# V's bound sent to all partitions by one matmul, and a new instruction order for attention and two MLPs

## The chip, the cores and the metric

The kernel runs on one core of a Trainium2 chip. The metric is device time in microseconds (us), from launch to end, as the median of several runs. The core has five engines with a queue each: TensorE (PE, matmuls), VectorE (DVE), ScalarE (ACT), GpSimd (POOL) and SyncE (SP, which here only starts transfers). Each works through its own instructions in program order and waits for the others by semaphores. PE's clock is granted by a throttle, at 1.2 or 2.4 GHz; the profile writes 0.5 and 1.0 for these.

## The reference

Attention with pooled queries, then an MLP with a leaky ramp, then an MLP with a rational function:

```python
q_pool = q.reshape(B, H, S // 2, 2, D).mean(axis=3)          # B=2, H=8, S=1152, D=64
scores = (1 / np.sqrt(D)) * np.matmul(q_pool, k.transpose(0, 1, 3, 2))
attn = np.exp(scores - scores.max(axis=-1, keepdims=True))
attn = attn / (attn.sum(axis=-1, keepdims=True) + 1e-09)
x = np.matmul(attn, v)                                        # -> 1152 tokens x 512
h = x @ w_in                                                  # 512 x 2048
x = (np.maximum(h, 0) + alpha * np.minimum(h, 0)) @ w_out     # 2048 x 512
h = x @ w_in2
P = a[0] + a[1] * h + a[2] * h**2 + a[3] * h**3
Q = 1 + abs(b[0]) * abs(h) + abs(b[1]) * h**2
out = (P / (Q + 1e-6)) @ w_out2
```

## The kernel before

**Numbers.** The matmuls keep nearly full float32 precision: an operand is split into a high part and a rest, and a product is three matmuls (high by high, high by rest, rest by high).

**Attention.** The 16 heads (2 batches of 8) run as 8 pairs `p`; head `2p` is the even one, `2p+1` the odd one. A head has 576 pooled queries and 1152 keys. For a pair, SP loads q, k and v (`load_q`, `load_k`, `load_v`); POOL adds the two query rows of a pool (`q_sum`) and forms a difference of keys (`k_diff`); ACT and DVE split q and k (`q_hi`, `q_lo`, `k_hi`, `k_lo`); SP's moves, all at L816, bring the parts to the tiles that PE reads: `qh_move` and `ql_move` into `QQ`, `k1_move` (two transfers) and `k2_move` into `K`. Then PE makes a first round of cheap scores for a bound on the maximum of each row (`max_mm`, with the parts `(p, j, chunks)`, read by `max_1` and `max_2` on DVE and `max_relu` on ACT; `max_split`, `max_rows` and `max_put` bring the bound back into `QQ`), and a second one for the scores themselves (`score n, t`, keys in 9 tiles `t`), which ACT exponentiates (`p_exp`, tile `PF`) and POOL or DVE splits (`p_lo`, tile `PL`). `av n, t` multiplies these with V, 15 matmuls at L1075, L1077 and L1079, into the bank `o` of head `n`; `norm` (L1088 to L1090) divides. `x_trans`, `x_hi` and `x_lo` carry the result to the MLP.

**V's bound.** V is scaled by a power of two that follows from its largest entry in the pair. `v_abs` (ACT) takes the largest absolute value per partition; `v_max` (PE, L899) turns this column into a row on one partition; `v_scale` (DVE, L904 to L909, five small operations) takes its maximum and makes the scale and its inverse there; `v_scale2` (PE, L912) multiplies by ones to have both on all 128 partitions, in PSUM; `v_scale3` (DVE, L917) copies them into the tile `vs`. `v_hi` (ACT) and `v_lo` (DVE, L938) make V's parts with it. For pairs 1 to 7 the row and the spread values lie behind the columns of head `2p-2`'s sum in its bank `o`; an `av` on that bank waits for DVE's read of it.

**The MLPs.** 512 model and 2048 inner dimensions; 16 f-tiles by three blocks of 384 tokens make 48 steps per MLP, `s` 0 to 47 and 48 to 95. A step is `mlp_in` (12 matmuls, L708), an elementwise part (MLP1: `act`, `prelu`; MLP2: `act`, `denom`, `denom2`, `numer`, `recip`, `newton`), the split `g_hi` (ACT) and `g_lo` (POOL, L1320), and `mlp_out` (9 matmuls, L1331). Weights arrive as 64-bit numbers and are made float32 by `w_abs`, `w_shift`, `w_top`, `w_low`, and split by `w_hi` (ACT) and `w_lo` (POOL, L680); MLP2's are made while its first token block runs. `mid_copy`, `mid_trans` and `mid_split` carry the result of MLP1 over, `last` that of MLP2 out.

**What sets the order.** No scheduler: every operation is entered with `at(time, function, ...)`, and `emit` calls all of them in the order of these times, which is the order in each engine's queue. The times come from a formula (a pair is 18 units, an MLP step 3.3) plus an entry of the table `NUDGE` under a key of the operation's name and time. A key with `+` holds for all pairs of the steady middle. In this kernel the table has some 510 entries, all for attention.

Of the kernel before, what the change touches and what calls it, by code (L numbers as in the profile page):

```python
# [21 lines left out]
P = 128  # L22

NUDGE = {
    "av +10.35": 0.124,
    "av +11.35": -0.146,
    "av +15.34": -0.123,
    "av +15.35": 0.109,
    "av +2.35": 0.223,
    "av +4.34": -0.294,  # L30
    "av +4.35": 0.851,
    "av +8.34": -0.854,
    "av +8.35": -0.053,
# [47 lines left out]
    "init_2 -59.70": -0.534,
    "init_3 -48.10": 9.574,
    "k1_move +7.30": -0.198,
    "k1_move +9.10": 2.890,
    "k1_move -47.27": 5.618,
    "k1_move -47.90": 4.202,
    "k1_move 11.70": 2.488,
    "k1_move 13.50": 1.398,
    "k2_move +0.36": 2.161,
    "k2_move +11.50": 0.543,  # L90
    "k2_move 108.36": 1.833,
    "k2_move 15.90": -0.539,
    "k2_move 8.10": -0.649,
    "k2_move 8.20": 1.103,
    "k_diff +6.50": 0.474,
    "k_diff -47.90": 0.005,
    "k_diff 10.90": -0.273,
    "k_hi +5.50": 0.667,
    "k_hi -47.90": -1.004,
    "k_hi 9.90": 0.525,  # L100
    "k_lo +10.00": 0.415,
    "k_lo 14.40": -1.147,
    "k_lo 7.04": -0.214,
    "load_k +13.00": -0.638,
    "load_k -59.98": 3.729,
    "load_k -59.99": 0.074,
    "load_k 1.50": 0.485,
    "load_k 13.00": -0.200,
    "load_q +13.00": 5.133,
    "load_q -59.97": 0.305,  # L110
    "load_q -60.00": -2.525,
    "load_q 1.50": 0.105,
    "load_q 13.00": 3.721,
    "load_v +13.00": -0.984,
    "load_v -59.96": 2.431,
    "load_v 0.69": 0.463,
    "load_v 13.00": 1.710,
    "max_1 +0.83": -0.321,
    "max_1 +10.86": 0.076,
    "max_1 +12.30": 0.259,  # L120
    "max_1 +2.27": -0.100,
    "max_1 +3.70": 0.078,
    "max_1 +8.00": -0.159,
    "max_1 -49.55": 0.073,
    "max_1 -50.55": 0.080,
    "max_1 -51.55": -0.390,
    "max_1 -52.55": -0.144,
    "max_1 -53.55": 0.216,
# [1338 lines left out]
```

## Time and profile before

| | us |
|---|---|
| time, median of 3 runs | 683.49 (682.04 to 684.49) |
| profiled execution | 685.3 |
| its span | 681.8 |
| PE busy | 646.8 |
| DVE busy | 515.9 |
| ACT busy | 484.5 |
| POOL busy | 402.7 |
| attention ends near | 268 |

The span runs from the first to the last instruction, and 3.5 us of the execution lie outside it. The mean granted clock of PE is 0.974. Busy time of PE counts matmuls as they run, so a matmul at half clock is busy for longer.

### The profile page before, as it was taken

How to read it: one execution, taken by the hardware profiler on the slowest of the kernel's cores; microseconds unless marked ns; L12 is line 12 of the kernel's file. 1: busy time of each engine (PE TensorE's matmuls, PEld its weight loads, DVE VectorE, ACT ScalarE, POOL GpSimd, SP SyncE). 2: the span in 40 equal slices, each digit the busy share in tenths (PEclk: the TensorE clock that was granted, in tenths of full speed). 3: DMA queues.
4: the chain of work that ended last, by engine and by line, in shares of the span. 5: the costliest groups of instructions: out<-in, count | busy, mean ns of one | idle time of the engine just before them, and what ended most of it. 6: DMA issues, size and time to landing. Idle time of an engine off the chain costs nothing.

```text
span 681.8 us, 13647 instructions
## 1 busy us (share of the span) xinstructions
PE 646.8 (95%) x5194; PEld 580.2 (85%) x5194; DVE 515.9 (76%) x949; ACT 484.5 (71%) x902; POOL 402.7 (59%) x353
## 2 busy tenths in 40 slices
PE   6798999799998889999999999999998999999997
PEld 5677999798897879999999999999887779999995
DVE  8887666769677998998992149996788877767774
ACT  5666687577867756666764368888788888778774
POOL 5554677567676775676664226785466655444442
PEclk8799799899999979999999999999999999999999
DMA  4778759595684224343331005640320010001001
GB/s 173 192 203 176 156 137 212 119 230 122 168 196 114 68 92 154 126 140 138 128 133 49 1 0 189 232 167 32 124 92 32 1 47 1 2 0 48 1 0 46
DMA packets 20960, 72.28 MB, mean 106 GB/s; under 512 B 3104, under 2 KB 3104, under 8 KB 20896
## 3 DMA queue, kind: packets, MB, share of 16 engines
q1 hardware_dynamic: 20896, 71.42, 37.3%
q8 instruction: 40, 0.66, 0.4%
q14 instruction: 24, 0.20, 0.1%
HBM read 47.72 MB, written 2.36 MB: 73 GB/s over the span
## 4 chain that ended last, share of the span: by engine, by line
PE 61%; DVE 19%; ACT 9%; issue 5%; DMA 4%; SPq 1%; POOL 1%; POOLq 0%; DVEq 0%; ACTq 0%
PE hp L708 20%; PE acc L1331 18%; PE st L1049 9%; PE m L962 5%; DVE bits L662 3%; PE o L1075 3%; PE o L1077 2%; PE o L1079 2%; DVE bits L657 2%; DMA QQ<-qh 2%; DVE ring L670 2%; DMA QQ<-qs 1%; DVE g L1312 1%; DVE g L1297 1%; DVE hp L1310 1%
## 5 line engine op out<-in xcount | busy, mean ns | idle before, releaser
L1063 POOL TENSOR_TENSOR PL<-PF 128x576 f16<-128x576 f32 x106 | 132.5, 1262 | 65.2 <-ACT PF L1057 64.0
L1320 POOL TENSOR_TENSOR gl<-g,gh 128x384 fp32r<-128x384 f32 x96 | 104.7, 1091 | 72.2 <-ACT gh L1316 58.2
L1057 ACT ACTIVATE PF<-st 128x576 f32<-128x576 f32 x144 | 91.4, 651 | 41.4 <-PE st L1049 35.1
L1331 PE MATMUL acc<-woh,gl 128*128 128x512 f32 x288 | 114.4, 397 | 3.2 <-POOL gl L1320 3.2
L1331 PE MATMUL acc<-woh,gh 128*128 128x512 f32 x288 | 113.3, 393 | 2.1 <-ACT m L1362 1.7
L1331 PE MATMUL acc<-wol,gh 128*128 128x512 f32 x288 | 113.2, 393 | 0.0
L1049 PE MATMUL st<-QQ,K 128*128 128x288 f32 (+1 forms) x576 | 107.8, 314 | 0.2
L1290 POOL TENSOR_TENSOR b<-a,b 128x384 f32<-128x384 f32 x48 | 48.9, 1018 | 84.5 <-ACT b L1278 83.3
L1049 PEld LDWEIGHTS st<-QQ,K 128*128 128x128 f32 (+1 forms) x576 | 90.6, 198 | 2.5 <-ACT PF L1057 0.8
L1075 PE MATMUL o<-V,PF 128*128 128x65 f16 x720 | 80.1, 197 | 11.2 <-DVE vs L917 6.9
L708 PE MATMUL hp<-xh,wih 128*128 128x384 f32 x384 | 83.7, 340 | 0.0
L708 PE MATMUL hp<-xl,wih 128*128 128x384 f32 x384 | 83.1, 338 | 0.0
L708 PE MATMUL hp<-xh,wil 128*128 128x384 f32 x384 | 83.0, 338 | 0.0
L962 PE MATMUL m<-K,QQ 128*128 128x384 f32 x234 | 73.8, 387 | 7.8 <-DMA QQ<-qh 2.7
L1075 PEld LDWEIGHTS <-PF 128*128 128x128 bf16 x720 | 67.8, 99 | 14.0 <-DVE x L1090 5.0
L1079 PE MATMUL o<-V,PL 128*128 128x65 f16 x720 | 78.7, 195 | 0.7 <-POOL PL L1063 0.6
L1077 PE MATMUL o<-V,PF 128*128 128x64 f16 x720 | 79.3, 198 | 0.0
L708 PEld LDWEIGHTS hp<-xh,wih 128*128 128x128 f32 x384 | 69.4, 188 | 7.6
L1077 PEld LDWEIGHTS <-PF 128*128 128x128 bf16 x720 | 69.0, 100 | 6.9 <-issue 6.9
L1316 ACT ACTIVATE gh<-g 128x384 fp32r<-128x384 f32 x96 | 49.9, 520 | 31.8 <-DVE g L1281 21.8
L1079 PEld LDWEIGHTS <-PL 128*128 128x128 f16 x720 | 68.9, 101 | 0.9 <-POOL PL L1063 0.7
L1331 PEld LDWEIGHTS acc<-woh,gl 128*128 128x128 f32 x288 | 54.1, 188 | 18.1 <-POOL gl L1320 6.7
(151 smaller groups left out, 1392.1 us busy)
## 6 DMA issues: line engine op xcount, KB each, us to landing
K<-kh SPq DMA_DIRECT2D x28, 384.0 KB, 6.2
ring<-in_w SPq DMA_DIRECT2D x19, 512.0 KB, 3.5
raw<-in_w SPq DMA_DIRECT2D x13, 512.0 KB, 3.5
ring<-in_w1o SPq DMA_DIRECT2D x10, 512.0 KB, 3.4
qr<-in_qT SPq DMA_DIRECT2D x8, 576.0 KB, 9.5
vr<-in_v SPq DMA_DIRECT2D x8, 576.0 KB, 9.1
ring<-in_w2o SPq DMA_DIRECT2D x9, 512.0 KB, 3.5
QQ<-qh SPq DMA_DIRECT2D x14, 288.0 KB, 5.0
```

The lines of the kernel that those rows point to most:

```text
L708: nc.tensor.matmul(hp, lhsT=w_[:, c * P:(c + 1) * P], rhs=x_[:, c, ts], start=k == 0, stop=k == 3 * KT - 1)
L962: nc.tensor.matmul(s[:, 0:CW], lhsT=of(QQ, n)[:, 0, k * P:(k + 1) * P], rhs=of(K1, n)[:, k0:k0 + CW], start=n == parts[0][0], stop=n == pa ...
L1049: nc.tensor.matmul(st[:, hf, 0:HALF], lhsT=k_[:, ks], rhs=q_[:, c:c + HALF], start=first, stop=not first)
L1057: nc.scalar.activation(out=PF[buf(n, t)][:, 0:SQ].rearrange("p (h q) -> p h q", h=2), in_=ST.pop((n, t))[:, :, 0:HALF], func=AF.Exp, scale=SC)
L1063: e.tensor_tensor(out=PL[u][:, 0:SQ], in0=PF[u][:, 0:SQ], in1=top(PF[u])[:, 0:SQ], op=ALU.subtract)
L1075: nc.tensor.matmul(o, lhsT=ph, rhs=V16[i][:, t, 0:D + 1], start=first, stop=False, skip_group_check=True)
L1077: nc.tensor.matmul(o[:, 1:D + 1], lhsT=ph, rhs=V16[i][:, t, D + 1:2 * D + 1], start=False, stop=False, skip_group_check=True)
L1079: nc.tensor.matmul(o, lhsT=pl, rhs=V16[i][:, t, 0:D + 1], start=False, stop=last, skip_group_check=True)
L1290: nc.gpsimd.tensor_tensor(out=E[u, "b"], in0=E[u, "a"], in1=E[u, "b"], op=ALU.mult)
L1316: nc.scalar.activation(out=G[u][0], in_=E[u, "g"], func=AF.Copy)
L1320: nc.gpsimd.tensor_tensor(out=gl, in0=E[u, "g"], in1=gh.bitcast(F32), op=ALU.subtract)
L1331: nc.tensor.matmul(acc, lhsT=g_[:, cs], rhs=w_, start=f == 0 and k == 0, stop=f == NF - 1 and k == 2)
```

## The change

It has two parts.

**V's bound.** `v_max` uses the column of maxima repeated 128 times as the weights, so that the row comes out on every partition. `v_scale` runs on 128 partitions and writes straight into the tile `vs`. `v_scale2`, `v_scale3` and the tile of ones go.

```diff
-        nc.tensor.matmul(AM[p, 1][0:1, VC:VC + P], lhsT=top(AM[p]), rhs=ident16, start=p == 0, stop=True,
-                         skip_group_check=True)
+        nc.tensor.matmul(AM[p, 1][:, VC:VC + P], lhsT=top(AM[p]).to_broadcast([P, P]), rhs=ident16,
+                         start=p == 0, stop=True, skip_group_check=True)
...
-        g = AM[p, 0] = small.tile([1, 8], F32, tag="g", name="g")
-        nc.vector.tensor_reduce(out=g[:, 0:1], in_=AM[p, 1][0:1, VC:VC + P], axis=AX.X, op=ALU.max)
+        g = small.tile([P, 5], F32, tag="vs", name="vs", bufs=3)
+        VS[p] = g[:, 3:5]
+        nc.vector.tensor_reduce(out=g[:, 0:1], in_=AM[p, 1][:, VC:VC + P], axis=AX.X, op=ALU.max)
...
-    def v_scale2(p):
-        nc.tensor.matmul(AM[p, 1][:, VC + P:VC + P + 2], lhsT=ones1, rhs=top(AM[p, 0])[:, 3:5], start=p == 0,
-                         stop=True, skip_group_check=True)
-
-    def v_scale3(p):
-        VS[p] = small.tile([P, 2], F32, tag="vs", name="vs", bufs=3)
-        nc.vector.tensor_copy(VS[p], AM[p, 1][:, VC + P:VC + P + 2])
...
```

**The order.** `NUDGE` is replaced by another table of some 330 entries, now with entries for the MLPs too; `where`, which makes the keys, gives one key to an operation in all steps of a stretch of an MLP:

```diff
+        s = (time - S2 * NP - 1) / 3.3
+        for i, (a, b) in enumerate(((5, 30), (35, 46), (51, 62), (66, 92))):
+            if a <= s < b:
+                return f"{fn.__name__} {i}"
...
-    "av +10.35": 0.124,
-    "av +11.35": -0.146,
...
```

What moves is seen in the engines' queues. At the start, the five `warm` matmuls ahead of the first `max_mm` of pair 0 stand behind its `max_mm 0,4`, ahead of `v_max 0`.

**SP, the transfers for pair 2** (`in_qT`, `in_kT` and `in_v` are the loads; `QQ_00` and `K1_00` belong to head 4, `QQ_12` and `K1_12` to head 5; `qh` and `qs` are the high and low part of q, `kh` the keys' high part, `ring` here the low part). Before:

```order
L816 DMA QQ_00_107<-qh_625 64x2x576
L813 DMA kr_721<-in_kT 128x1152
L816 DMA QQ_00_107<-qs_601 64x576
L816 DMA K1_00_102<-kh_632 64x1536 x2
L928 DMA vr_796<-in_v 128x1152
L816 DMA K1_12_106<-kh_632 64x1536 x2
L816 DMA QQ_12_111<-qs_601 64x576
L816 DMA K2_00_112<-ring_80 64x1152
L807 DMA qr_867<-in_qT 128x1152
L816 DMA QQ_12_111<-qh_625 64x2x576
L816 DMA K2_10_114<-ring_80 64x1152
```

After:

```order
L632 DMA kr_606<-in_kT 128x1152
L635 DMA K1_00_102<-kh_608 64x1536 x2
L626 DMA qr_707<-in_qT 128x1152
L635 DMA QQ_00_107<-qh_651 64x2x576
L635 DMA QQ_00_107<-qs_646 64x576
L635 DMA QQ_12_111<-qh_651 64x2x576
L739 DMA vr_779<-in_v 128x1152
L635 DMA QQ_12_111<-qs_646 64x576
L635 DMA K1_12_106<-kh_608 64x1536 x2
L635 DMA K2_00_112<-ring_80 64x1152
L635 DMA K2_10_114<-ring_80 64x1152
```

The `qh` move of head 5 goes from the last place but one to the sixth, `load_q 3` from the ninth to the third, and the first `qh` move stands behind `load_k 3` and the first key moves. In the pairs that follow, `load_q` stands ahead of `load_k` and both `k2` moves, where it stood behind `load_k` and one of them.

**DVE, around `v_scale 4`** (`junk` and `nm` with ISA is `max_2`, `nm<-m` is `max_1`, `PL<-PF` a `p_lo`, `V_1` the odd head's V). Before:

```order
L976 ISA nm 128x1
L904 TENSOR_REDUCE g<-o 1x1
L905 TENSOR_SCALAR g<-g 1x1
L906 TENSOR_SCALAR g<-g 1x1
L908 TENSOR_SCALAR g<-g 1x1
L909 RECIPROCAL g<-g 1x1
L938 SCALAR_TENSOR_TENSOR V_1_117<-vr,vs,V_1_117 128x9x64
L971 TENSOR_REDUCE nm<-m_2284 128x1
L1063 TENSOR_TENSOR PL_124<-PF_118 128x576
L917 COPY vs<-o 128x2
```

After:

```order
L787 ISA nm 128x1
L749 SCALAR_TENSOR_TENSOR V_1_117<-vr,vs,V_1_117 128x9x64
L725 TENSOR_REDUCE vs<-o 128x1
L726 TENSOR_SCALAR vs<-vs 128x1
L727 TENSOR_SCALAR vs<-vs 128x1
L729 TENSOR_SCALAR vs<-vs 128x1
L730 RECIPROCAL vs<-vs 128x1
L782 TENSOR_REDUCE nm<-m_2262 128x1
L787 ISA junk_2313,nm<-m_2309,relu 128x384
```

`v_lo 7` stands ahead of `v_scale 4`, and `max_2` ahead of the `p_lo` that stood between `v_scale` and `v_scale3`.

**POOL, MLP2's first token block** (`b<-a,b` is `denom2`, `gl` `g_lo`, `wol` and `wil` `w_lo` of the outer and inner weights). Before:

```order
L1290 TENSOR_TENSOR b1_4453<-a1_4451,b1_4453 128x384
L680 TENSOR_TENSOR wol10_5081<-m2_4463,woh10_5080 128x512
L1320 TENSOR_TENSOR gl1_4460<-g1_4455,gh1_4459 128x384
L1290 TENSOR_TENSOR b0_4452<-a0_4450,b0_4452 128x384
L1320 TENSOR_TENSOR gl2_4462<-g2_4456,gh2_4461 128x384
L680 TENSOR_TENSOR wil13_5091<-ring_80,wih13_5090 128x512
```

After:

```order
L1101 TENSOR_TENSOR b1_4413<-a1_4411,b1_4413 128x384
L1131 TENSOR_TENSOR gl1_4420<-g1_4415,gh1_4419 128x384
L1101 TENSOR_TENSOR b0_4412<-a0_4410,b0_4412 128x384
L1131 TENSOR_TENSOR gl2_4422<-g2_4416,gh2_4421 128x384
L501 TENSOR_TENSOR wol10_5055<-m2_4423,woh10_5054 128x512
L1101 TENSOR_TENSOR b1_4413<-a1_4411,b1_4413 128x384
```

`w_lo` of the outer weights of f-tile 10 stood ahead of the `g_lo` of its step and now stands behind two of them. On ACT the `w_abs` and `w_hi` of this block stand earlier within a step, and `last 0,0` stands ahead of a `g_hi`. In the tail of attention, `norm 13` stands ahead of the `w_shift` that it stood behind.

## Rows read from the trace of the kernel before

**Rows 1.** The page: busy us, share of the span and instructions of each engine.

```profile
PE 646.8 (95%) x5194; PEld 580.2 (85%) x5194; DVE 515.9 (76%) x949; ACT 484.5 (71%) x902; POOL 402.7 (59%) x353
```

**Rows 2.** PE's waits: who waited for whom, us in total, times, longest us.

```profile
PE o L1075 <- DVE vs L917: 6.9, 6, 3.6
PE o L1075 <- DVE x L1090: 4.3, 3, 2.6
PE acc L1331 <- POOL gl L1320: 3.2, 7, 1.0
PE m L962 <- DMA QQ<-qh: 2.7, 1, 2.7
...
PE vt L899 <- ACT junk L889: 2.3, 1, 2.3
```

**Rows 3.** Stretches: length, busy us (instructions) by engine, granted clock, DMA share, GB/s.

```profile
55.90:66.50 10.60, 9.13 (x130) 8.27 (x128) 7.89 (x23) 7.03 (x14) 4.97 (x4) 1.00 0.94 180
66.50:76.70 10.20, 8.76 (x78) 7.99 (x79) 3.98 (x9) 4.45 (x7) 6.55 (x6) 0.50 0.41 84
...
131.30:134.70 3.40, 3.17 (x27) 2.94 (x27) 2.29 (x6) 0.88 (x2) 1.12 (x1) 0.50 0.86 175
...
240.50:247.40 6.90, 6.31 (x72) 6.17 (x73) 6.11 (x9) 3.04 (x6) 4.38 (x6) 0.51 0.23 76
247.40:300.00 52.60, 51.65 (x452) 47.19 (x452) 49.80 (x61) 34.54 (x65) 35.10 (x26) 1.00 0.37 131
300.00:500.00 200.00, 199.72 (x1020) 181.25 (x1019) 144.65 (x211) 136.53 (x258) 113.04 (x95) 1.00 0.32 109
500.00:552.00 52.00, 47.15 (x226) 39.52 (x224) 43.72 (x78) 43.08 (x82) 31.50 (x30) 1.00 0.09 31
```

**Rows 4.** Timeline of SP's queue, pair 2: start us, us, engine, line, transfer.

```profile
42.10 0.62 SPq L816 DMA_DIRECT2D QQ<-qh  x1
...
44.46 1.16 SPq L816 DMA_DIRECT2D K<-kh  x2
...
54.61 1.07 SPq L816 DMA_DIRECT2D QQ<-qh  x1
```

**Rows 5.** The page's transfers: count, KB each, median us from issue to landing.

```profile
K<-kh SPq DMA_DIRECT2D x28, 384.0 KB, 6.2
...
QQ<-qh SPq DMA_DIRECT2D x14, 288.0 KB, 5.0
```

**Rows 6.** Timeline of PE: start us, us, instruction [idle before it <- who ended that].

```profile
67.69 0.66 PE L962 MATMUL m<-K,QQ 128*128 128x384 f32 x1 [2.66 <-DMA QQ<-qh]
...
125.77 0.21 PE L1075 MATMUL o<-V,PF 128*128 128x65 f16 x1
...
131.53 0.21 PE L1075 MATMUL o<-V,PF 128*128 128x65 f16 x1 [3.60 <-DVE vs L917]
...
517.80 0.50 PE L1331 MATMUL acc<-woh,gl 128*128 128x512 f32 x1 [1.03 <-POOL gl L1320]
...
551.96 0.50 PE L1331 MATMUL acc<-woh,gh 128*128 128x512 f32 x1 [1.66 <-ACT m L1362]
```

**Rows 7.** Timeline of DVE, pair 4 and the tail.

```profile
124.96 0.27 DVE L904 TENSOR_REDUCE g<-o 1x1 f32<-1x128 f32 x1
...
129.91 1.50 DVE L1063 TENSOR_TENSOR PL<-PF 128x576 f16<-128x576 f32 x1 [1.71 <-POOL PL L1063]
131.34 0.15 DVE L917 COPY vs<-o 128x2 f32<-128x2 f32 x1
...
238.78 1.36 DVE L657 TENSOR_SCALAR m<-m 128x512 int32<-128x512 int32 x1
```

**Rows 8.** The tile `vs`: `v_lo`, ns min/median/max, first and last start.

```profile
L938 DVE SCALAR_TENSOR_TENSOR V<-vr,vs,V x16: 791/810/1864, 26.5 to 245.6; 128x576 f16<-128x576 f32 x16
```

**Rows 9.** Timeline of POOL, pair 4 and MLP2.

```profile
125.71 1.41 POOL L820 TENSOR_TENSOR qs<-qr 128x576 f32<-128x576 f32 x1 [3.97 <-DMA K<-ring]
...
515.50 1.28 POOL L680 TENSOR_TENSOR wol<-ring,woh 128x512 fp32r<-128x512 f32 x1
```

More of the change, by code (lines that the diff above doesn't have):

```diff
@@ L81 @@
[L81 to L116, printed above, removed]
@@ new lines @@
+    "k_diff +6.50": 0.25928,
+    "k_diff -47.90": -0.31042,
+    "k_hi +5.50": 0.65607,
+    "k_hi -47.90": -1.70901,
+    "k_hi 9.90": 0.20816,
+    "k_lo +10.00": 0.05122,
+    "k_lo 14.40": -1.33281,
+    "last 3": -0.73145,
+    "last 472.04": 5.6109,
+    "load_k +13.00": 2.48384,
+    "load_k -59.98": 1.81846,
+    "load_k 13.00": -2.94287,
+    "load_q +13.00": 2.46736,
+    "load_q -59.97": 0.51382,
+    "load_q 13.00": -0.67075,
+    "load_v +13.00": 0.92681,
+    "load_v 0.69": 0.27781,
@@ new lines @@
+    "p_lo 124.05": 0.04433,
+    "p_lo 128.05": -0.03096,
+    "p_lo 129.05": 0.35293,
+    "p_lo 135.05": -0.11243,
+    "p_lo 17.05": 0.76834,
+    "p_lo 5.05": -0.42349,
+    "prelu 1": 0.06312,
+    "prelu 160.51": -0.19632,
+    "prelu 252.91": -0.76034,
+    "prelu 302.41": 0.19939,
+    "q_hi +6.40": -0.79569,
+    "q_hi 10.80": 0.14579,
+    "q_lo +7.40": -0.4857,
+    "q_lo 0.57": -3.22216,
+    "q_lo 11.80": 0.12554,
+    "q_sum -48.20": -1.59167,
+    "q_sum -56.59": 0.04284,
+    "q_sum 9.60": 1.13451,
@@ new lines @@
+    "v_abs 112.00": 0.5906,
+    "v_hi +14.96": -2.44725,
+    "v_hi +5.19": 0.12102,
+    "v_hi 1.97": -0.0338,
+    "v_hi 122.96": -0.05458,
+    "v_hi 14.96": 0.46325,
+    "v_lo +5.92": 0.08909,
+    "v_lo 123.69": -0.0255,
+    "v_max +5.40": 0.37337,
+    "v_max -47.98": 1.78699,
+    "v_max 9.38": 0.15233,
+    "v_scale +5.60": 0.4134,
+    "v_scale -47.78": 3.71659,
+    "v_scale 113.60": 0.27805,
+    "w_abs 1": 0.08196,
+    "w_abs 132.54": -0.19784,
+    "w_abs 153.93": 0.30825,
+    "w_abs 157.06": 0.44095,
@@ new lines @@
+    "w_shift 300.53": 0.17955,
+    "w_shift 351.35": -0.14967,
+    "w_top 0": 0.51732,
+    "w_top 115.14": 0.76013,
+    "w_top 118.92": -0.77142,
+    "w_top 130.25": -0.2934,
+    "w_top 141.59": 0.95071,
+    "w_top 152.53": 0.36648,
+    "w_top 155.67": 0.44095,
+    "w_top 158.80": 0.44095,
+    "w_top 2": 0.01244,
+    "warm -47.99": 0.14036,
+    "warm -58.62": 1.87459,
+    "x_hi +16.29": -0.36444,
+    "x_hi 124.29": -0.41997,
+    "x_hi 142.29": -0.2355,
+    "x_hi 149.50": 0.35742,
@@ L764, in init_1 @@
         make_identity(nc, ident)
-        nc.gpsimd.memset(ones1, 1.0)
     def warm(n):
@@ L909, in v_scale, with v_scale_at @@
         nc.vector.reciprocal(out=g[:, 4:5], in_=g[:, 3:4])
[L911 to L923 removed]
+    def v_scale_at(time, p):
+        at(time, v_max, p)
+        at(time + 0.2, v_scale, p)
     def load_v(p):
```

739 lines of the change are left out of this document (259 added, 480 removed).

## The prediction

> **What bounds the kernel now.** I read the busy times first. TensorE (PE) is busy 646.8 of the 681.8 us span, so at most 35 us of idle time are there to be won, and a part of that is the start and the end [rows 1]. An engine that is busy 95% of the time still loses where it stands still and where its clock is halved, so the next two views were the list of PE's waits and a table by stretches with the granted clock [rows 2, 3]. The list names a few large waits: 6.9 us in six waits for the copy `vs` that `v_scale3` writes (L917), 4.3 us in three waits for `norm` (L1090), 3.2 us in seven waits for `gl`, one wait of 2.7 us for a transfer into `QQ`, one of 2.3 us before the first `v_max` [rows 2]. The table adds what the list can't say: behind three of these waits the granted clock is 0.50 (1.2 GHz instead of 2.4 GHz), for 10.2 us from 66.5, 3.4 us from 131.3 and 6.9 us from 240.5 [rows 3]. In 300 to 500 us PE is busy 199.72 of 200 us: nothing to win in MLP1 and the start of MLP2. In 500 to 552 us it is busy 47.15 of 52 [rows 3]. So the time lies in attention (up to 268 us) and in the first token block of MLP2.
>
> **The sum's base.** All terms come from the profiled execution: a span of 681.8 us and 3.5 us outside it, 685.3 us. The median of the runs, 683.49, is 1.8 us below that. Gains are taken off the median. A measurement of this kernel can tell about 0.3%, 2 us, from no change.
>
> **The edit of V's bound.** Eight `v_scale2` matmuls, eight `v_scale3` copies and one memset go. The matmuls are small beside PE's full queue and I count nothing for them; the copy takes 0.15 us [rows 7], 1.2 us of DVE in all. `v_max` now loads a repeated column and writes 128 partitions instead of one, and `v_scale`'s five small operations run on 128 partitions. The trace has no such reduce; the nearest rows are the reduce on one partition, 0.27 us, and the copy on 128 partitions, 0.15 us [rows 7], so I take no change, with 0 to 0.3 us per pair as bounds. What matters is the chain, and it is shorter by a matmul, a copy and two hand-overs.
>
> **A: operands of pair 2.** The last operand for the `max_mm` at 64.70 arrives so late that PE waits 2.66 us, until 67.69; it is the `qh` move, issued at 54.61 behind the whole rest of the group [rows 4, 6]. Then the clock is half for 10.2 us, which costs 5.1 [rows 3]. The new SP order puts `qh_move 5` ahead of `load_v 2`; last of what this `max_mm` needs is now `k1_move 5`, and only the two `K<-ring` moves of 288 KB stand behind it. So one to two transfers of 288 KB [rows 5] fewer lie ahead of PE's need: at the 180 GB/s of this stretch [rows 3] 1.6 to 3.2 us. The wait falls to between 0 and 1.1. I take 0.6 and expect the clock to hold: a gain of 2.1 + 5.1 = 7.2 at PE, of which I count 5.0, since the operands of pair 3 are the next late thing. Low end 1.5 (the clock falls all the same), high end 7.8. The price that the order pays: `qh_move 4`, issued at 42.10, now stands behind `k1_move 4`, which couldn't go before 44.46 [rows 4]; with `load_k`, two 384 KB moves and `load_q` ahead it should land near 53, and PE needs it at 55.9. That cover is 3 us; if it is gone, each us late is a us lost.
>
> **The start.** Five `warm` matmuls move behind `max_mm 0,4`, so that they lie in the 2.3 us hole before `v_max` [rows 2]. Whatever PE gains here is, in the trace of before, taken back by the transfers at 55.9 to 67.7. I count 0, and 2.3 as the upper bound.
>
> **B: pairs 3 to 7.** Gross, the waits for `vs` are 6.9 us, and the longest, 3.60 at 131.53, is followed by 3.4 us at half clock, 1.7 lost [rows 2, 3, 6]: 8.6. The chain of the longest: the copy stood on DVE behind a `p_lo` that waited 1.71 us for POOL, and POOL had waited 3.97 us with `q_sum 5` for a DMA [rows 7, 9]. Two things change. The copy is gone, so PE no longer asks for it. And SP issues `load_q` ahead of `load_k` and the second `k2` move instead of behind them, which is worth about 576 + 288 KB or some 3 to 4 us, so of the 3.97 I leave 0.8. In its place comes **a new wait**: `v_lo` of the odd head now stands ahead of `v_scale` on DVE. Any `av` behind `v_max` in PE's order that writes the same bank must wait until `v_scale`'s reduce has read it. In pair 4 the reduce ran at 124.96 and the `av` at 125.77 [rows 6, 7]. `v_lo` takes 0.79 to 1.86 us [rows 8]: with 1.86 ahead the reduce ends at 127.09, 1.3 late; with 0.81 it ends at 126.04, 0.3 late. The move of the last `max_mm` of `max 3` ahead of an `av` lets DVE start some 0.4 earlier. Over five pairs (2 to 6) I take 1.4 in all, bounds 0 and 6.5. Net 8.6 - 1.4 - 0.8 = 6.4, with bounds 1.0 and 8.6.
>
> **A rule on that price.** The Trainium skill's GPSIMD Engine Reference (section 1, Specifications) says that GpSimd's SBUF interfaces are shared with VectorE, and that DVE instructions with two SBUF inputs contend; `v_lo` has two. The trace agrees in part: the median is 810 ns and the longest 1864 [rows 8]. By that rule `v_lo` would be long wherever POOL is at work, which is the last rival below.
>
> **C: the tail, 203 to 268 us.** `norm 13` stood behind a `w_shift` of 1.36 us [rows 7]; now it runs first. The longest of the three waits for `norm`, 2.6 us [rows 2], shrinks to about 1.3; what this stretch lost to the last copy is within B's 6.9. The half clock that follows costs 3.4 [rows 3]. But DVE is busy 49.80 of 52.60 us there [rows 3], and what is put ahead of one thing is put behind another. I take 2.0: 1.3 and a part of the clock; bounds 0.5 and 4.8.
>
> **D: MLP2's first block.** PE waits for `gl` 3.2 us in seven waits, none over 1.0 us [rows 2]; the one at 517.80 comes just after POOL ran a `w_lo` of 1.28 us ahead of the `g_lo` [rows 6, 9]. The new order puts `w_lo` behind `g_lo` and lifts ACT's weight operations into its gaps. A wait of 1.0 is covered by 1.28, so I take 2.4 of the 3.2. `last 0,0` moves ahead of a `g_hi` on ACT; of the 1.66 wait at 551.96 [rows 6] I take 1.1. Together 3.5, bounds 1.0 and 4.9 (all of the idle in 500 to 552 [rows 3]). At the passage from MLP1 to MLP2 some copies on ACT come later; PE's cover there is the full stretch of 300 to 500 us [rows 3], so 0, and 2 if that lead is gone.
>
> **The sum.** 5.0 + 6.4 + 2.0 + 3.5 = 16.9; 683.5 - 16.9 = 666.6 us (span about 665). The low ends add up to 4.0 (679.5 us), the high ends, with the start, to 28.4 (655 us). All terms don't reach one end at once.
>
> **Rivals.**
> *The clock still falls.* Waits of up to 1.66 us in 500 to 552 us left the clock at 1.00, and those of 2.6 to 3.6 us in attention were followed by 0.50 [rows 2, 3, 6]. If the shorter waits that I leave in A, B and C still bring the half clock, 5.1 + 1.7 + 0.7 less is won, partly counted already in A's discount: about 673. For it: 55.9 to 66.5 is no dense stretch, PE is busy 9.13 of 10.60 [rows 3]. Against it: 500 to 552 is no denser. The Trainium skill's TensorE: Matmul & The Clock Gate (What's actually happening) says that the gate is set by how busy the array has been of late; read so, one wait less does not keep the clock, and the time would be this rival's, 673.
>
> *Attention doesn't move.* The transfers and DVE set attention's pace, and what PE wins at one place it waits at the next. For it: DVE's 95% in 247 to 300 us [rows 3]. Against: the longest wait of a pair ended on a chain of copy, `p_lo`, `q_sum` and DMA that the change cuts at both ends [rows 7, 9]. Then only D counts: 680.
>
> *Slower, by `v_lo` ahead of `v_scale`.* If `v_lo` takes 1.86 us in each of five pairs and the 1.3 us wait brings the half clock each time, at 1.7 to 5.1 us (mean 3.4) as after the waits in before [rows 3], the loss is 5 x 4.7 = 23.5. Against it stand 5.0 + 8.6 - 0.8 + 2.0 + 3.5 = 18.3: 688.7. It decides from 3.7 us a pair, so not without the clock.
>
> *All of it.* Every clock fall avoided and nothing late behind: 655.
>
> **Chances.** The forecast 0.60; the clock still falls 0.14; attention doesn't move 0.10 (half of it within 0.3%); slower by `v_lo` 0.08; all of it 0.08. So faster by over 0.3%: 0.60 + 0.14 + 0.08 + 0.05 = 0.87; within 0.3%: 0.05; slower: 0.08. The range leaves out the slower rival, the lower half of the last and the far half of the one at 680: 657 to 681.
>
> **What would show it.** Right, if in the profile of after PE waits nowhere for `vs` over 1 us, the stretch after `max_mm 2,4` has a granted clock of 1.00, POOL's `q_sum` waits under 1.5 us, and PE's idle in MLP2's first block falls under 2 us. B's price is seen in PE's waits of `av` for the reduce of `v_scale`, A's in a wait for `QQ<-qh` at the start of pair 2. It is wrong if a new wait of over 2 us with a half clock behind it stands in several pairs, or if `q_sum` and the first `max_mm` of a pair still wait for transfers.

## The result and the profile after

The changed kernel takes 662.17 us (median of 4 runs, 661.50 to 663.11), the kernel before 683.24 beside it: a ratio of 0.969, with a 95% interval of 0.967 to 0.972. That is 21 us, where the forecast said 16.9 (666.6 us). The profiled span went from 681.8 to 660.8 us.

Busy times of the engines, from the page of after (the line that answers to [rows 1]):

```profile
PE 634.4 (96%) x5186; PEld 573.3 (87%) x5186; DVE 502.0 (76%) x941; ACT 486.1 (74%) x902; POOL 410.8 (62%) x352
```

PE's busy time fell by 12 us with only eight matmuls fewer; matmuls at half clock count double in it, and there are fewer of them now. The mean granted clock went from 0.974 to 0.990, which is some 35 us at half clock in before and some 13 in after. The one profile of before lies at an end, though: in the 31 runs of before beside the experiments the clock was 0.977 to 0.990 (677.4 to 686.5 us), so a part of this difference is that profile's own. By place, before has 13.7 us of it in the start and after 3.4, with another 3.4 in pair 1; that part can have given no more than the 0.8 us by which after leads at pair 2 (the marks below).

PE's waits (who waited for whom, us in total, times, longest):

```profile
PE o L886 <- DVE x L901: 2.9, 1, 2.9
PE m L773 <- issue: 2.5, 1, 2.5
...
PE m L773 <- DVE mt L805: 1.7, 1, 1.7
PE mtp L1159 <- DVE xl L1165: 1.4, 1, 1.4
...
PE m L773 <- DMA QQ<-qs: 1.1, 1, 1.1
...
PE acc L1142 <- POOL gl L1131: 0.8, 3, 0.3
...
PE acc L1142 <- ACT m L1173: 0.7, 1, 0.7
```

Of the large waits of [rows 2], the 6.9 us for `vs` are gone, the 2.7 us for `QQ<-qh` too, and `gl` and `last` (`m`, L1173) fell from 4.9 to 1.5. One of the three waits for `norm` (L901) is still there, at 2.9 instead of 2.6 us. New are a wait of 2.5 us ahead of the first `max_mm` of pair 1 and one of 1.7 us for `mt` later in that pair; at the passage from MLP1 to MLP2 (`mid_trans`, L1159) PE waits 1.4 us, in before 0.3.

The stretches of after (length, busy us of PE, PEld, DVE, ACT, POOL, granted clock, DMA share, GB/s):

```profile
31.40:36.00 4.60, 4.58 (x45) 3.92 (x45) 2.82 (x7) 3.21 (x6) 2.10 (x2) 0.70 1.04 294
55.10:83.10 28.00, 26.84 (x387) 24.32 (x388) 20.18 (x51) 20.36 (x38) 18.35 (x15) 1.00 0.82 189
83.10:109.70 26.60, 26.43 (x390) 24.27 (x389) 20.21 (x51) 20.87 (x39) 20.79 (x18) 1.00 0.78 185
216.20:233.00 16.80, 12.70 (x178) 11.74 (x174) 15.98 (x23) 9.58 (x18) 13.43 (x11) 0.80 0.28 97
...
480.50:531.00 50.50, 49.70 (x247) 44.05 (x245) 43.71 (x77) 43.35 (x82) 33.00 (x31) 1.00 0.09 32
```

The second and third lines are pairs 2 and 3: full clock, and in pair 3 PE is busy 26.43 of 26.60 us. Pairs 4 to 6 take the same 26.6 us. The last line answers to 500 to 552 us of before, mostly MLP2's first block, with 0.8 us of idle time instead of 4.9 [rows 3].

The ledger is best read from marks: the time at which PE starts the same piece of work in both timelines, and after's lead over before.

| mark (start on PE) | before | after | lead | gained since the last mark | forecast |
|---|---|---|---|---|---|
| first `max_mm` of pair 1 | 33.87 | 31.42 | 2.5 | 2.5 | 0 (start) |
| of pair 2 | 55.89 | 55.14 | 0.8 | -1.7 | 0 |
| of pair 3 | 89.79 | 83.11 | 6.7 | 5.9 | 5.0 (A) |
| of pair 7 | 203.22 | 189.47 | 13.8 | 7.1 | 6.4 (B) |
| first `mlp_in` | 260.69 | 244.61 | 16.1 | 2.3 | 2.0 (C) |
| first `mlp_in` of MLP2 | 460.17 | 444.06 | 16.1 | 0 | 0 |
| `mlp_in` of MLP2's second block | 533.48 | 514.18 | 19.3 | 3.2 | |
| of its third block | 603.67 | 583.17 | 20.5 | 1.2 | 3.5 (D, both) |
| end | 681.8 | 660.8 | 21.0 | 0.5 | 0 |

All four terms came out within their bounds and within 1 us of the value taken. Whether they came out for the stated reasons is another question, and the experiments say that some did not.

### The profile page after: what moved, and what is told of

The parts are those of the page before. It is cut to its first block, busy times and chain, and to the rows that moved or that the text cites. A ratio compares the mean times of both kernels' runs of the same rounds, so it can differ in the third digit from the quotient of the medians.

```text
span 660.8 us, 13617 instructions
## 1 busy us (share of the span) xinstructions
PE 634.4 (96%) x5186; PEld 573.3 (87%) x5186; DVE 502.0 (76%) x941; ACT 486.1 (74%) x902; POOL 410.8 (62%) x352
## 5 line engine op out<-in xcount | busy, mean ns | idle before, releaser
L874 POOL TENSOR_TENSOR PL<-PF 128x576 f16<-128x576 f32 x106 | 137.7, 1314 | 58.0 <-ACT PF L868 54.1
L860 PE MATMUL st<-QQ,K 128*128 128x288 f32 (+1 forms) x576 | 103.5, 306 | 0.9 <-ACT PF L868 0.8
L1101 POOL TENSOR_TENSOR b<-a,b 128x384 f32<-128x384 f32 x48 | 48.9, 1019 | 78.2 <-ACT b L1089 78.2
L860 PEld LDWEIGHTS st<-QQ,K 128*128 128x128 f32 (+1 forms) x576 | 87.5, 192 | 2.9 <-ACT PF L868 1.5
L773 PE MATMUL m<-K,QQ 128*128 128x384 f32 x234 | 71.6, 372 | 10.4 <-issue 2.5
L886 PE MATMUL o<-V,PF 128*128 128x65 f16 x720 | 78.4, 196 | 2.9 <-DVE x L901 2.9
L890 PE MATMUL o<-V,PL 128*128 128x65 f16 x720 | 77.1, 194 | 1.3 <-DVE PL L874 0.9
L888 PE MATMUL o<-V,PF 128*128 128x64 f16 x720 | 77.7, 197 | 0.0
L886 PEld LDWEIGHTS <-PF 128*128 128x128 bf16 x720 | 67.2, 98 | 11.9 <-DVE x L901 3.1
L529 PEld LDWEIGHTS hp<-xh,wil 128*128 128x128 f32 x384 | 68.7, 188 | 0.0
L529 PEld LDWEIGHTS hp<-xl,wih 128*128 128x128 f32 x384 | 68.6, 188 | 0.0
```

Of the source, the lines that this page charges most:

```text
L529: nc.tensor.matmul(hp, lhsT=w_[:, c * P:(c + 1) * P], rhs=x_[:, c, ts], start=k == 0, stop=k == 3 * KT - 1)
L773: nc.tensor.matmul(s[:, 0:CW], lhsT=of(QQ, n)[:, 0, k * P:(k + 1) * P], rhs=of(K1, n)[:, k0:k0 + CW], start=n == parts[0][0], stop=n == pa ...
L860: nc.tensor.matmul(st[:, hf, 0:HALF], lhsT=k_[:, ks], rhs=q_[:, c:c + HALF], start=first, stop=not first)
L874: e.tensor_tensor(out=PL[u][:, 0:SQ], in0=PF[u][:, 0:SQ], in1=top(PF[u])[:, 0:SQ], op=ALU.subtract)
L886: nc.tensor.matmul(o, lhsT=ph, rhs=V16[i][:, t, 0:D + 1], start=first, stop=False, skip_group_check=True)
L888: nc.tensor.matmul(o[:, 1:D + 1], lhsT=ph, rhs=V16[i][:, t, D + 1:2 * D + 1], start=False, stop=False, skip_group_check=True)
```

## The experiments

The letters A to D are the forecast's terms. The kernels of a set ran on the same chip, those of the first set on another one than those of the second and third. There the kernel before took 680.67 us (first set), 680.78 (second), 682.14 (third), and after, run again in the second set alone, 661.75, which is 19.0 less. Sizes are read against those, so across sets they are good to 1 or 2 us; intervals are 95%. Stages of single profiles repeat better from pair 3 on: where the order is the same, pairs 3 to 6 (from `v_max 3` to `v_max 7` on PE) take 106.0 to 106.1 us in nine profiles, and the tail (from there to the first `mlp_in`) 47.6 to 47.8 in nine.

### The edit without the order, and the order without the edit

`edit_alone` is before with

```diff
-        nc.tensor.matmul(AM[p, 1][0:1, VC:VC + P], lhsT=top(AM[p]), rhs=ident16, start=p == 0, stop=True,
+        nc.tensor.matmul(AM[p, 1][:, VC:VC + P], lhsT=top(AM[p]).to_broadcast([P, P]), rhs=ident16,
...
-        at(t2, v_scale2, p)
-        at(t2 + 0.2, v_scale3, p)
```

> The kernel before in its old order, with the new v_max and v_scale and without v_scale2 and v_scale3. Theory (the 6.9 us of waits for vs and the 1.7 us of half clock behind the longest were the copy's place in the queues; the late q_sum and the late transfers stay): PE waits nowhere for vs, pairs 3 to 7 gain 3 to 6 us, pair 2's wait for the qh transfer of 2.7 us and the half clock behind it stay: 677 to 680 us. Rival 1 (the order is all of the gain, the edit only opens it): 682 to 684, with the same time lost to PL or the m banks. Rival 2 (the edit does all of pairs 3 to 7): 675 to 676.

Measured: 680.95 us, ratio 0.999 (0.995 to 1.002). The first rival, and a miss for the theory. The waits for `vs` are gone indeed, and yet the pairs are no shorter. Pairs 3 to 6 take 115.9 us, in before 113.8. PE stands at half clock for 6.8 us of that, from 100.8, and for 3.4 us in before; taking half of that off as its cost leaves 112.5 and 112.1, so the clock doesn't hide a gain.

```profile
100.80:107.60 6.80, 6.70 (x54) 5.99 (x51) 4.21 (x9) 2.18 (x4) 3.71 (x3) 0.50 0.92 199
```

POOL's `q_sum` in its timeline says why (start us, us, [idle before it <- who ended that]):

```profile
152.32 1.42 POOL L818 TENSOR_TENSOR qs<-qr 128x576 f32<-128x576 f32 x1 [2.75 <-issue]
...
180.60 1.42 POOL L818 TENSOR_TENSOR qs<-qr 128x576 f32<-128x576 f32 x1 [2.88 <-issue]
```

One `q_sum` follows another after 27.6 to 29.8 us, much as in before. What each waits for is its `load_q`, although the list says `issue` (nothing that the profile shows): the landing, which the trace has for every transfer, is 0.1 to 0.2 us ahead of each. The last `load_q` of edit_alone goes out at 170.95 and lands at 180.48. In SP's and POOL's timelines, edit_alone, then before, then after:

```profile
170.95 1.21 SPq L805 DMA_DIRECT2D qr<-in_qT  x1
```

```profile
173.86 0.50 SPq L807 DMA_DIRECT2D qr<-in_qT  x1
182.90 1.42 POOL L820 TENSOR_TENSOR qs<-qr 128x576 f32<-128x576 f32 x1 [1.91 <-issue]
```

```profile
156.15 1.82 SPq L626 DMA_DIRECT2D qr<-in_qT  x1
167.87 1.41 POOL L639 TENSOR_TENSOR qs<-qr 128x576 f32<-128x576 f32 x1
```

The four rounds between the last five `q_sum` of each trace (us):

| | `q_sum` to the next `load_q` going out | to its landing | to the next `q_sum` | round |
|---|---|---|---|---|
| before | 17.5 to 19.8 | 8.9 to 11.0 | 0.1 to 0.2 | 27.9 to 30.9 |
| edit_alone | 18.2 to 19.5 | 9.2 to 10.1 | 0.1 to 0.2 | 27.6 to 29.8 |
| after | 14.9 to 15.2 | 7.3 to 7.9 | 3.8 to 4.4 | 26.6 to 26.7 |

So in before and in edit_alone it is the round of a pair (load, `q_sum`, split, moves, then the next loads) that sets the pace, and it takes longer than PE's 26.6 us. With the copy gone PE waits for something else in it: `max_mm` for the reads of the `m` banks, 3.7 us in six waits between 66 and 200 us. The chain that the profile follows back shows the way there: from the `q_sum` at 180.60 by ACT's `k_hi` and DVE's `max_2`, `q_lo` and `max_1` to the `max_mm` at 187.42. The six waits:

```profile
PE m L952 <- DVE nm L961: 1.4, 3, 0.8
PE m L952 <- DVE nm L966: 1.3, 1, 1.3
PE m L952 <- ACT relu L958: 1.0, 2, 0.6
```

In after the operand of `q_sum` is there some 4 us early, and `q_sum` stands at 88.11, 114.66, 141.27 and 167.87, 26.6 apart, without a wait.

`order_alone` is after with the old four steps; the last two stand where they stood in before.

```diff
+    def v_scale3(p):
+        VS[p] = small.tile([P, 2], F32, tag="vs", name="vs", bufs=3)
+        nc.vector.tensor_copy(VS[p], AM[p, 1][:, VC + P:VC + P + 2])
...
+        at(t2, v_scale2, p)
+        at(t2 + 0.2, v_scale3, p)
```

> The kernel after with the old v_max, v_scale, v_scale2 and v_scale3, the last two at the places they had before. Theory (with load_q early, DVE's queue is no longer held by a late p_lo, so the copy costs little in most pairs): PE waits for vs 0.2 to 0.7 us in each of seven pairs, 663.5 to 667 us. Rival 1 (the edit was most of B's 7 us): 668 to 670 us. Rival 2 (the order alone): 662 to 663 us.

Measured: 668.37 us, ratio 0.981 (0.976 to 0.986); after alone had 0.973 (0.970 to 0.976) in the second set. So the edit is worth some 6 us on top of the new order (6.6 by the medians, 5.4 by the ratios), and nothing on top of the old one. PE's waits for `vs` in order_alone, 60 to 200 us and 195 to 260 us:

```profile
PE o L907 <- DVE vs L749: 1.4, 5, 0.3
...
PE o L907 <- DVE vs L749: 1.3, 1, 1.3
```

That is 2.7 us. Its pairs 2 to 6 take 27.4 us instead of 26.6, 0.9 longer each, with only 0.3 of it in the waits; its tail takes 48.9 instead of 47.7. The rest of the 0.9 lies in matmuls that I had counted at nothing. From PE's timeline in pair 4, order_alone ahead of after:

```profile
121.22 0.19 PE L911 MATMUL o<-V,PL 128*128 128x65 f16 x1
121.34 0.22 PE L731 MATMUL o<-ident,am 128*1 128x128 f16 x1
121.49 0.40 PE L881 MATMUL st<-QQ,K 128*128 128x288 f32 x1
...
124.84 0.17 PE L744 MATMUL o<-g,ones 1*128 1x2 bf16 x1
124.94 0.61 PE L794 MATMUL m<-K,QQ 128*128 128x384 f32 x2
```

```profile
117.33 0.19 PE L890 MATMUL o<-V,PL 128*128 128x65 f16 x1
117.36 0.22 PE L718 MATMUL o<-ident,am 128*128 128x128 f16 x1
117.39 0.38 PE L860 MATMUL st<-QQ,K 128*128 128x288 f32 x1
...
120.64 0.51 PE L773 MATMUL m<-K,QQ 128*128 128x384 f32 x2
```

The `v_max` of one column starts 0.12 us after the matmul ahead of it, and the next one 0.15 us after that; with 128 columns both are 0.03 us. So the wider one is the cheaper one. Laid side by side, matmul by matmul, the pair is 0.89 us longer in order_alone: 0.21 at `v_max`, 0.31 at `v_scale2` and the `max_mm` right behind it, 0.44 at the wait (0.28 of it idle), less 0.07 elsewhere.

### What cured pair 2

`sp_pair2_back` is after with SP's transfers for pair 2 in the order of before.

```diff
+    "qh_move 12.00": -1.0,
...
+    "load_q 13.00": 3.721,
+    "qh_move 13.55": 4.756,
```

> The kernel after with SP's transfers for pair 2 in the order of before, nothing else moved. Theory (A: this order alone made PE wait 2.7 us at 64.7 and brought the half clock of 10 us): a wait of 2 to 3 us for QQ<-qh near 62 to 65, a stretch of about 10 us at a granted clock of 0.5 behind it, the mark of the first max_mm of pair 3 some 5 to 7 us later, 667 to 669 us. Rival 1 (the wait comes back, the clock does not fall): 664 to 665. Rival 2 (pair 2 gained elsewhere, by POOL's or ACT's order): 662 to 663.

Measured: 665.22 us, ratio 0.976 (0.971 to 0.981). Between the theory and its first rival: pair 2 takes 29.6 us from `v_max` to `v_max` instead of 26.6, but the wait for `QQ<-qh` is 0.8 us, and no half clock follows. The first `ql` move goes out at 24.10 us there, as in after, and at 26.45 in before. So a new theory: the start, which the forecast had counted at 0, does part of A. `start_back` puts the order of before into the start on all engines, `start_sp_back` both.

```diff
...
+    "qh_move -47.43": 2.164,
...
+    "v_abs -49.53": 0.752,
...
+    "warm -48.74": -5.568,
...
```

> The kernel after with the order of before up to the first steps of pair 0 (on all engines), the rest as in after. With only pair 2's transfers put back, the wait for QQ<-qh was 0.8 us and no half clock followed, so I now think that the earlier start of the transfers (the first ql move issued at 24.1 us, not 26.4) did a good part of A. Theory 2 (start and SP order each would do for pair 2): the lost lead of 2.4 us is taken back at the first max_mm of pair 2 as in before, the wait at pair 2's max_mm stays under 1 us, no half clock: 662 to 664. Rival (the start is worth its 2.4 us and a wait in pair 2 comes back): 665 to 668.

Measured: 662.53 us, ratio 0.975 (0.972 to 0.978), not to be told from after's 661.75 beside it; pair 2 takes 26.6 us. Theory 2 as far as it goes: the start alone is worth nothing that these runs can tell.

> The kernel after with both the start and SP's transfers for pair 2 as in before. Theory 2: now the wait of 2 to 3 us for QQ<-qh is back near 63 to 65 us, the granted clock behind it falls to 0.5 for 3 to 10 us, and pair 3 starts 4 to 7 us later than in after: 666 to 669 us. Rival (what cured pair 2 is the edit or POOL's order inside the pair): the wait stays under 1 us, 662 to 665.

Measured: 667.18 us, ratio 0.980 (0.977 to 0.984), 5.4 us above after. Put back one by one the start and pair 2's order cost 0.8 and some 3, together 5.4. Of that, 3.3 us lie in pair 2, from `v_max` to `v_max`, and the rest ahead of it, where two profiles of after differ by 2.4. So 3.3 of A's size is shown to be the order of the transfers. But neither the wait nor the clock came back as I had said. PE's waits between 55 and 80 us and the stretch in which before stood at half clock:

```profile
PE m L895 <- DMA QQ<-qh: 1.4, 1, 1.4
PE m L895 <- DVE nm L904: 1.0, 1, 1.0
```

```profile
65.00:70.00 5.00, 3.62 (x52) 3.09 (x52) 3.80 (x13) 2.60 (x6) 2.22 (x2) 1.00 0.43 84
```

Pair 2 takes 29.8 us there, 29.9 in edit_alone, and 33.4 in before. Edit_alone had nearly before's wait, 2.3 us for `QQ<-qh`, and this clock behind it:

```profile
65.00:70.00 5.00, 2.87 (x34) 2.59 (x34) 1.88 (x6) 2.27 (x4) 3.70 (x4) 0.66 0.11 24
70.00:75.00 5.00, 5.00 (x58) 4.69 (x56) 4.44 (x9) 3.38 (x7) 3.79 (x4) 1.00 0.63 128
```

A mean of 0.66 over 5 us is 3.4 us at 0.50 and the rest at 1.00; these are all of it, where [rows 3] show 10.2 us of it behind a wait of 2.7. So some 3.5 us of what I booked under A, the difference between 33.4 and 29.9, were the length that the half clock happened to have in the one profile of before.

### The pairs: `load_q` and `v_lo`

`load_q_late` is after with `load_q` behind `load_k` and the first `k2` move again, `v_lo_behind` with `v_lo` of the odd head behind `v_scale`.

```diff
+    "load_q +13.00": 5.133,
```

> The kernel after with load_q of pairs 4 to 7 back behind load_k and the first k2 move. Theory (B: the early load_q is what frees q_sum and with it POOL, DVE and PE): q_sum waits 2 to 4 us for a transfer in each pair, and pairs 3 to 6, now 26.6 us each, take 27 to 28.5: 664 to 669 us. Rival (PE has slack enough, since the copy that made PE wait for DVE is gone): POOL waits, PE doesn't, 662 to 663 us.

Measured: 664.51 us (662.49 to 667.29), ratio 0.976 (0.970 to 0.983). The runs scatter too much for 2 us. In its profile three `q_sum` wait again, for 0.3 to 0.8 us, and the pairs from 3 on take 27.1, 26.8, 27.3 and 26.3 us: 1.4 us more in all than in after. Both lie between the theory and the rival. `load_q` lands 0.1 to 0.4 us ahead of `q_sum` there, in rounds of 26.5 to 27.3 us. So the rest of the order had already brought the round from 28 to 30 us down to about PE's pace, and the early `load_q` gives it some 4 us to spare: by its own size a small part of B.

```diff
+    "v_lo +5.92": 0.12,
```

> The kernel after with v_lo of the odd head behind v_scale in the pairs of the steady middle, as it stood in before. The forecast priced v_lo's place ahead of v_scale at 1.4 us in all (0 to 6.5); the trace of after shows no wait of an av for vs over 0.3 us. Theory (v_lo ahead costs PE nothing, since the reduce still ends before the av): 661.5 to 663 us, pairs of 26.6 us. Rival (it costs the small wait of some 0.3 us that stands at each v_max): 660 to 661.5, pairs of 26.3.

Measured: 662.10 us, ratio 0.973 (0.971 to 0.976), against after's 661.75 in the same set. The theory: `v_lo` ahead costs nothing; its profile has the same 26.6 us a pair. DVE in pair 4 of after, and PE's `av`:

```profile
117.68 0.82 DVE L749 SCALAR_TENSOR_TENSOR V<-vr,vs,V 128x576 f16<-128x576 f32 x1
118.41 0.28 DVE L725 TENSOR_REDUCE vs<-o 128x1 f32<-128x128 f32 x1
118.73 0.15 DVE L726 TENSOR_SCALAR vs<-vs 128x1 f32<-128x1 f32 x1
```

```profile
118.75 0.19 PE L886 MATMUL o<-V,PF 128*128 128x65 f16 x1
```

The reduce ends at 118.69, the `av` starts at 118.75, and no wait is put down to it. The price I gave the wide reduce, 0.27 us, is 0.28. What I had not seen is the margin: `v_max` to `av` is 1.4 us in PE's queue, and DVE needs 0.8 + 0.3 of it.

### The tail

`norm13_behind` puts `norm 13` behind the `w_shift` again. `norm13_first` tries to get rid of its wait: on DVE `norm 13` and `p_lo 14,1` go ahead of `w_low 0,1,o`; it also puts `mid_trans 2,2` behind `mlp_out(1,0,1)`, where PE waits 1.4 us at 464.

```diff
+    "norm 128.76": 0.6,
```

> The kernel after with norm 13 again behind w_shift 0,2,i on DVE, as it stood in before. The forecast gave the move 1.3 us and a part of the clock. In the trace of after the w_shift takes 0.61 us, and the wait for norm 13 is 2.9 us, longer than in before. Theory now (the move is worth its 0.6 to 1.4 us and no clock): 662.5 to 663.5 us. Rival (PE's wait there is set by the p_lo and the weight steps ahead of both, and made up behind): 661.5 to 662.3.

```diff
+    "norm 128.76": -0.392,
+    "p_lo 128.05": 0.34,
+    "w_low 127.63": 1.17,
...
-                    at(e + 3.3 * (1.2 + 0.5 * c), mid_trans, T, c)
+                    at(e + 3.3 * (1.2 + 0.5 * c) + (0.06 if c == 2 else 0.0), mid_trans, T, c)
```

> The kernel after with two waits of the trace of after taken on: on DVE norm 13 and then p_lo 14,1 stand ahead of the last step of the weight w_low 0,1,o (they stood behind it, and PE waits 2.9 us for norm 13 near 222 us, with half clock behind it); on PE mid_trans 2,2 stands behind mlp_out(1,0,1) and not right behind mid_trans 2,1 (a wait of 1.4 us at 464). Theory (both waits are only a matter of order): the wait for norm 13 falls under 0.5 us, one of 0.5 to 1.2 us for the PL of p_lo 14,1 takes its place, no half clock in the tail, 1 to 1.5 us saved at 464: 657 to 659.5 us. Rival 1 (DVE is full in the tail, so what is put first is paid for by the weight behind it; the lead at 464 is taken back in MLP2's first block): 661 to 663 us. Rival 2 (only the clock comes back): 659.5 to 661.

Measured: norm13_behind 662.66 us, ratio 0.972 (0.968 to 0.976); norm13_first 663.72 us, ratio 0.975 (0.971 to 0.978). Neither differs from after beyond the intervals. The profiles are clearer: from `v_max 7` to the first `mlp_in` before takes 49.5 us, after 47.8 (47.6 in its second profile), norm13_behind 48.7, norm13_first 48.7, against 47.6 to 47.8 in all nine profiles with after's tail. PE's waits in the tail, of norm13_behind and then of norm13_first:

```profile
PE o L890 <- DVE x L905: 4.9, 2, 4.3
```

```profile
PE st L866 <- ACT PF L874: 2.8, 2, 2.0
PE o L896 <- DVE PL L880: 2.3, 3, 0.9
PE o L892 <- DVE x L907: 0.6, 1, 0.6
```

With `norm 13` ahead of its `w_shift` the wait is 2.9 (after), behind it 4.3: the move is worth 1.4 us at that wait, as the forecast had it, though only 1.0 by the mark. Made earlier still, the wait for `norm` all but goes and comes back as waits for `PF` and `PL`; of the half clock behind it 3.4 us are left, where after has 6.8. The first rival holds for it: DVE is busy 4.90 to 4.97 of every 5 us from 205 to 230 us in after, and what goes first is paid for by what stands behind. The second change in norm13_first went the same way. MLP2's first half block (to its ninth step) took 34.8 us instead of 36.4, the second half 35.6 instead of 33.7: the lead was taken back where the elementwise chain sets the pace.

### MLP2's first block

`mlp2_order_back` drops all entries from the end of MLP1 on, `w_lo_ahead` only the one for `w_lo`.

```diff
+for _k in ("act 255.26", ..., "mlp_in 2", ..., "w_abs 2", ..., "w_hi 2", ..., "w_lo 2", ...):
+    NUDGE.pop(_k, None)
...
+for _k in ("w_lo 2", ):
+    NUDGE.pop(_k, None)
```

> The kernel after without any entry of the new table from the end of MLP1 on (steps 30 and later), so in the order of before there. Theory (D and the end are worth 4.4 and 0.5 us, the passage from MLP1 to MLP2 costs 1.1): PE waits for gl about 3 us and for last 1.7 us again, no wait of 1.4 us at mid_trans 2,2: 665 to 667 us. Rival (part of the gain there comes with attention's earlier end, since weights arrive at the same pace): 662.5 to 664.5 us.

> The kernel after with only the one entry removed that puts POOL's w_lo behind g_lo in MLP2's first block; ACT's new places stay. Theory of the forecast (w_lo ahead of g_lo is what PE waited for): waits for gl of 2 to 3 us again, 664 to 665.5 us. Rival (ACT's order was it: with the elementwise chain ahead by some 3 us, g_lo has slack for a w_lo): waits for gl under 1.3 us, 661.5 to 662.8 us.

Measured: mlp2_order_back 667.30 us, ratio 0.979 (0.975 to 0.983), some 5 us above after; in the profiles it is 5.2 from the first `mlp_in` of MLP2 to the end. w_lo_ahead 661.36 us, ratio 0.972 (0.968 to 0.976), no different from after. PE's waits between 440 and 560 us in the first:

```profile
PE acc L1145 <- POOL gl L1134: 3.0, 6, 1.0
PE acc L1145 <- ACT m L1176: 1.7, 1, 1.7
```

and between 470 and 560 in the second:

```profile
PE acc L1145 <- ACT m L1176: 0.7, 1, 0.7
PE acc L1145 <- POOL gl L1134: 0.5, 2, 0.3
```

So the gain is the order's, not a gift of attention's earlier end, and the place of `w_lo`, on which the forecast rested D, is not the cause: with `w_lo` ahead of `g_lo` again PE waits for `gl` as little as in after. What remains are the places of ACT's `w_abs`, `w_hi` and `g_hi`, and of the matmuls and copies. ACT's own waits point to the first, 480 to 530 us, mlp2_order_back and then w_lo_ahead:

```profile
ACT hp L1117 <- DVE g L1111: 4.1, 6, 1.2
```

```profile
ACT hp L1117 <- DVE g L1111: 1.4, 3, 0.8
```

`hp` is the second half of `recip`, in the chain that goes to and fro between ACT, DVE and POOL. No run singled this out, so ACT's part is argued, not shown.

`after_again` is the kernel after once more, unchanged.

> The kernel after, unchanged, beside the other kernels of this set on the same chip: 662 us, and the same marks of the pairs to within 1.5 us. If the first max_mm of pairs 2 and 3 shift by more than that, what the single profiles say of the start and of pair 2 is too rough for a size.

Measured: 661.75 us, ratio 0.973 (0.970 to 0.976). Its pairs lie 2.4 us earlier than in the first profile from pair 2 on (and 1.0 in pair 1), with the same 26.6 us each. So the start of one profile is good to 2 us only, and what single profiles say of the first 60 us is rough; pair against pair is good to 0.1 in this order.

## Why the prediction was right, and where its steps were not

The sum was near (16.9 against 21.0 us, 19.0 in the second set), and so was the forecast's reading that the time lay at a few places in attention and MLP2. All four of its signs came: no wait for `vs`, a clock of 1.00 in pair 2, no `q_sum` that waits over 1.2 us, and 0.8 us of idle time in MLP2's first block. That the terms came out one by one is in part luck: in A, B and D what the forecast named was not, or only in part, what won. By its steps:

- **V's bound.** "I count nothing for them" was wrong for the matmuls. The one-column `v_max` cost 0.21 us a pair more than the wide one, and `v_scale2` 0.31. In the new order, where PE is the bound in the pairs, the edit is worth some 6 us. In the old order it is worth nothing, since there the round of the transfers is longer than PE's work. The price of the wide reduce was right.
- **A** was right in size (5.9 between the marks of pairs 2 and 3), and the forecast's cure, the order of the transfers, is confirmed by sp_pair2_back and start_sp_back for some 3 us of it. Another 3.5 is the length of the half clock in one profile of before, so that part is luck. Three of its numbers failed. The half clock, 5.1 of its 7.2, did not come back in pair 2 in either run. The start, counted at 0, may be part of the cure: the runs put 0.8 us on it alone, no more than they can tell. And the cover of 3 us for `qh_move 4` and `ql_move 4` wasn't there in after's first profile: PE waits 1.1 us for `QQ<-qs` at the start of pair 2, and not at all in after_again.
- **B** was right in size (7.1 against 6.4), and wrong in its working. The step that failed is the one that books the waits for `vs` as time to be won by the edit: edit_alone won all of them and no time, because `q_sum` stood right behind the landing of `load_q` and the round took 28 to 31 us, with or without them. The forecast had this chain in hand, in the `q_sum 5` that waited 3.97 us, and took it for one late transfer and not for the pace. The new order brought the round down to PE's 26.6; `load_q_late` shows that the early `load_q` gives the slack and that other moves had done most of it, and which of those is not shown. The price of `v_lo` ahead of `v_scale`, 1.4, was 0, by v_lo_behind: in pairs 2 to 6 of after that `v_lo` took 0.82 us and not up to 1.86. (By its own terms the low end of B is 1.3 and not 1.0.) Of the rivals, "attention doesn't move" describes what the edit alone does.
- **C** was right in size (2.3 against 2.0), half in its reason. The move of `norm 13` gave its 1.0 to 1.4, but against a wait that had grown; the wait is 2.9 us in after and the half clock behind it is still there, 0.80 in the mean over 216 to 233 us. Where the rest, about 1 us, comes from stays open: from the mark of pair 7 to the first `mlp_in` PE's idle time fell by 0.9 us only and its busy time by 1.5, at a mean clock of 0.94 in both.
- **D** was right in size (4.4 and 0.5 at the end, against 3.5), and PE's waits for `gl` and `last` fell by 2.4 and 1.0 us, as forecast; but the place of `w_lo`, which it named as the cause, isn't it, and what the cause is stays open. The passage from MLP1 to MLP2, counted at 0, cost 1.1.
- **The rivals.** "The clock still falls" was in part what happened in the start and the tail, without costing what was feared. One of its reasons was a misreading: 55.9 to 66.5 us looks no dense stretch because it holds half of the wait. Up to the wait PE was busy all the time, and the clock fell behind it all the same:

```profile
55.90:65.03 9.13, 9.13 (x130) 8.27 (x128) 6.71 (x19) 7.03 (x14) 4.97 (x4) 1.00 1.03 197
```

  The slower one failed at its first step, the long `v_lo`.

## What to carry to other kernels

A wait in the list is time to be won only if nothing else runs at the same pace: measure the period of the whole round (here from one `q_sum` to the next), look whether an operation in it stands right behind a landing each time, and compare it with the busy time of the engine that is to become the bound, before adding up waits. A small edit can be worth nothing in one order and 1% in another, so the two are to be run apart and together. In a stretch where an engine is busy 98% of the time, as DVE in the tail, moving one operation forward shifts the wait to another.

## What the runs showed of the hardware

- The half clock behind a wait of PE is not a fixed price. Waits of 2.7 and 2.3 us in pair 2 were followed by 10.2 and some 3.4 us of it. The same wait of 2.1 to 2.5 us ahead of pair 1, in two profiles of the same kernel, is followed by a granted clock of 0.70 in after and of 1.00 in after_again over the same stretch:

```profile
31.40:36.00 4.60, 4.17 (x49) 3.64 (x49) 2.88 (x8) 3.52 (x7) 2.29 (x2) 1.00 1.02 306
```

  In after_again the clock falls later: a wait of 1.74 us for `mt` ends at 43.48 there and at 44.51 in after. PE is busy without a break behind both, at half clock for 3.4 of 5 us in after_again and at full clock in after (after_again, then after):

```profile
43.50:48.50 5.00, 5.00 (x48) 4.29 (x49) 3.74 (x7) 1.72 (x4) 0.95 (x1) 0.66 0.98 245
```

```profile
44.50:49.50 5.00, 5.00 (x64) 4.29 (x65) 4.69 (x10) 2.90 (x7) 0.98 (x1) 1.00 0.96 230
```

  So an estimate from one profile should carry the clock's part in its range and not in its sum.
- A matmul whose stationary operand is one column wide, with 128 moving columns, was followed by the next one after 0.15 us and followed the one ahead of it after 0.12, between full-width matmuls at full clock; the same with the column repeated 128 times took 0.03 and 0.03.
- `v_lo`, which reads two tensors on DVE, took 0.79 to 0.81 us in the eight cases of before in which POOL did nothing meanwhile, and 1.60 to 1.86 in four in which POOL was busy for most or all of it. But one that POOL's work covered wholly took 0.92, and in after those of the steady pairs took 0.82 with POOL busy for up to 0.67 us of it. So POOL at work doesn't by itself make it long.
